# A fused recurrence, Fourier mixing and MLP kernel: the last row tile in two column parts, under new order tables

## The chip, the cores and the metric

The kernel runs on one core of one Trainium2 chip. A core has a matrix engine (PE, TensorE) whose weight loads (PEld) overlap its matmuls, a vector engine (DVE), a scalar engine (ACT), a general engine (POOL, GpSimd) and a queue engine (SP) that here issues transfers only. Matmul results go to eight PSUM banks. The metric is the device time of one execution in microseconds, the median of several runs.

## The reference

Four batches, eight heads, 768 time steps, 48 channels for each head, all in fp32. First a recurrence for each head, then a two-dimensional Fourier transform of which the real part is kept, a normalisation and a two-layer MLP with a residual.

```python
for t in range(S):
    kt, vt, rt, wt = (k[:, :, t].copy(), v[:, :, t].copy(), r[:, :, t].copy(), w[:, :, t].copy())
    cur = np.einsum('bhd,bhe->bhde', u[None] * kt, vt)
    y[:, :, t] = np.einsum('bhd,bhde->bhe', rt, state + cur)
    state = wt[:, :, :, None] * state + np.einsum('bhd,bhe->bhde', kt, vt)
...
X = np.fft.fft(x, axis=1)
X = np.fft.fft(X, axis=2)
mixed = np.real(X).astype(np.float32)
u = x + mixed
mu = np.mean(u, axis=-1, keepdims=True)
var = np.mean((u - mu) ** 2, axis=-1, keepdims=True)
un = (u - mu) / np.sqrt(var + 1e-06)
ch = np.maximum(un @ w_ch1, 0.0) @ w_ch2
return (u + ch).astype(np.float32)
```

## The kernel before

The work is written as a list of small operations, each with a kind and a number (`rl` 17 is the 18th ReLU). `op` (L63) records an operation with what it reads and writes; waits follow from that. Two tables then fix where and when it runs. `PLACES` holds a string of digits for some kinds: the digit at place n picks one of the engines that the call offers for operation n. `PLAN` holds a key for every operation; `schedule` (L100) sorts each engine's operations by key, and that is the engine's instruction order, so a key is a place in a queue and every engine works its queue strictly in order. `schedule` also walks through the orders once to give each PSUM tile a bank (L143 to L148): a bank is handed on when the last operation on its tile is through. `emit` (L194) sets the waits and, at the end, lets DVE wait for every output store (L261 to L265).

A batch has six chunks of 128 steps. `load` issues on SP the tiles w, k, r, v of a chunk (192 KB each, load number 4 x chunk + 0 to 3); `weights` issues the two MLP weight matrices on POOL (`wgt` 0 for W1, 1 for W2, L697 and L698), tied to a load of chunk 5.

`attention` works on one chunk: ACT takes logarithms (`Ln`) and exponentials (`ex`, `ew`, L739) of cumulative sums from PE (`tce`, `tci`); products go to POOL or DVE (`rk`, `rku`, `vtd`, `kh`) or read a bank on DVE (`rh`); `vb` casts v to bf16; PE transposes (`trr`, `trk`), the results are copied out by ACT or DVE (`rT`, `kT`, L785 and L786); PE forms the 128 x 128 products (`am`), DVE masks them (`ms`, L802); PE forms the state and the output (`sm`, `y`, for chunks 0 to 5 with the diagonal term by `yx`, L830), DVE scales the state (`st`), and `xc` copies the output out (L853, L854). `fe`, `fo` (L867, L870) fold the channels for the transform.

`mix` works on a batch: PE transforms along the sequence with 193 columns at a time (`sq`, L897), the results are copied (`hc`, L914 and L915, and `hr` from those); PE transforms along the channels (`dm`), DVE adds the input (`uf`, L955), takes statistics (`bs`, `ba`), `un` centres, PE transposes (`tr`), `ut` copies out. For batches 2 and 3 two of the six row tiles are mirrored by transfers instead, and `uf` is a sum of two SBUF tiles there, on DVE or POOL. Then, for each half batch q of three row tiles, 12 `m1` (three matmuls of 384 columns each, L998) with a ReLU each on ACT or DVE (`rl`, L1003 and L1004) make the hidden layer HT, and for each row tile three `m2` (four matmuls each, L1014) accumulate over the 12 blocks of HT into one bank. `ob` (L1020) scales by the inverse deviation and adds the residual on DVE, and `out` (L1024) stores the 192 KB tile from SP. Row tile 23 is the last of the run: its three `m2` are the last instructions of PE, its `ob` the last of DVE and its `out` the last transfer.

Until its real work is dense, PE is kept busy by matmuls on a zero tile (`beat`, L1040), 29 at the start and others in gaps that `fill_gaps` finds in the walk of `schedule`.

Of the kernel before, what the change touches and what calls it, by code (L numbers as in the profile page):

```python
# [7 lines left out]
ALU = mybir.AluOpType  # L8
# [24 lines left out]
class _Prog:  # L33
# [254 lines left out]
    def _topo(self):  # L288
# [3 lines left out]
        while n < len(self.ops):  # L292
# [18 lines left out]
    "tce": [2, 6, 17, 14, 32, 39, 67, 112, 81, 111, 153, 161, 170, 189, 203, 245, 246, 260, 275, 283, 325, 317, 338, 375],  # L311
    "tci": [3, 4, 8, 12, 34, 37, 49, 94, 92, 105, 145, 160, 171, 184, 199, 212, 234, 263, 272, 287, 343, 318, 329, 372],
    "tot": [7, 5, 10, 18, 36, 58, 97, 96, 110, 147, 175, 185, 200, 213, 242, 280, 288, 345, 327, 336],
    "trr": [9, 16, 22, 23, 43, 56, 76, 126, 116, 141, 165, 172, 183, 197, 222, 252, 268, 270, 285, 298, 361, 357, 367, 397],
    "trk": [13, 11, 20, 25, 47, 50, 71, 130, 122, 146, 164, 178, 192, 194, 235, 243, 255, 286, 305, 306, 360, 359, 364, 394],
    "sm": [15, 31, 40, 48, 64, 86, 131, 154, 168, 179, 187, 210, 254, 271, 284, 307, 322, 358, 386, 399],
    "am": [19, 24, 33, 30, 57, 62, 82, 137, 132, 151, 174, 182, 196, 204, 240, 257, 274, 296, 352, 311, 368, 370, 385, 401],
    "set": [0, 1, 4, 3, 5, 6, 5, 11, 13, 21, 23, 1, 2, 16, 22, 25, 28, 3, 4, 26, 27, 30, 34, 5, 6, 7, 14, 35, 19, 40, 18, 32,
           33, 50, 36, 45, 51, 41, 57, 39, 24, 12, 29, 17, 31, 21, 28, 27],
    "yx": [26, 38, 42, 44, 59, 66],  # L320
    "y": [29, 41, 45, 51, 65, 70, 129, 152, 150, 167, 181, 190, 207, 244, 262, 278, 292, 304, 373, 339, 374, 389, 398, 406],
    "beat": [35],
# [64 lines left out]
    "wgt": [28, 36],  # L387
    "ix": [47, 84],
    "dx": [88],
    "mg": [110, 109, 125, 124],  # L390
# [711 lines left out]
```

## Time and profile before

| | us |
|---|---|
| median of 3 runs | 192.83 (192.76 to 192.97) |
| the profiled execution | 193.89 |
| its span, first to last instruction | 192.1 |

| engine | busy us | share of the span | instructions |
|---|---|---|---|
| PE | 182.9 | 95% | 1803 |
| PEld | 120.9 | 63% | 1803 |
| DVE | 163.8 | 85% | 405 |
| ACT | 139.9 | 73% | 326 |
| POOL | 106.9 | 56% | 130 |

The profile is of one execution, whose own time stands beside its span; the span starts with the first instruction and leaves out what lies around it. Times in the views count from the start of the span. A row of the grouped view reads: line, engine, operation, output from inputs, shapes, count, then busy us and mean ns of one, then the idle time of the engine ahead of them and what ended it. The view by stretches gives the busy time of each engine in a stretch with the instruction count in brackets, then the clock granted to PE, DMA's mean share and its GB/s. The view of the chain that ended last gives start, length and what ran.

### The profile page before, as it was taken

The page shows a single profiled execution, that of the slowest core. Times are in us where ns is not written, and L with a number is a line of the kernel's source. Part 1 is how long each engine was busy: PE and PEld are TensorE (multiplying, and loading weights), DVE is VectorE, ACT ScalarE, POOL GpSimd, SP SyncE. Part 2 cuts the span into 40 slices and gives each one's busy share as a digit, 9 for nine tenths or more (in the row PEclk, how much of TensorE's full clock was granted, in tenths as well). Part 3 has the DMA queues.
Part 4 walks back from the last instruction along what each step waited for, and adds up shares of the span by engine and source line. Part 5 has one row for each costly group of instructions (what it writes and reads, how often), then busy time and mean ns, then how long its engine had stood idle before and what let it go on. Part 6 is the DMA issues. An engine that isn't in the chain of part 4 may idle for free.

```text
span 192.1 us, 4796 instructions
## 1 busy us (share of the span) xinstructions
PE 182.9 (95%) x1803; PEld 120.9 (63%) x1803; DVE 163.8 (85%) x405; ACT 139.9 (73%) x326; POOL 106.9 (56%) x130
## 2 busy tenths in 40 slices
PE   7798999998899999999999999999999999999993
PEld 5465668845567666767667577665666676666561
DVE  8698999899989999999999989898989947584532
ACT  4896997879988468879999777878875766473410
POOL 3139665745907967994999794694992301200000
PEclk9999999999999999999999999999999999999999
DMA  5998999999999896999979990156601022203303
GB/s 120 211 190 157 201 195 182 188 210 196 174 184 180 175 198 149 201 230 194 232 169 223 193 217 19 46 163 171 160 0 44 2 85 82 82 0 126 125 0 123
DMA packets 106109, 27.84 MB, mean 145 GB/s; under 512 B 100387, under 2 KB 105510, under 8 KB 106086
## 3 DMA queue, kind: packets, MB, share of 16 engines
q1 hardware_dynamic: 103878, 24.39, 59.1%
q0 software_dynamic: 2208, 3.15, 8.9%
q8 instruction: 14, 0.23, 0.5%
q14 instruction: 9, 0.07, 0.1%
HBM read 24.38 MB, written 5.51 MB: 156 GB/s over the span
## 4 chain that ended last, share of the span: by engine, by line
PE 76%; SPq 10%; DVE 8%; DMA 2%; issue 1%; ACT 1%; POOL 0%; DVEq 0%; POOLq 0%
PE bank L1014 24%; PE bank L998 22%; SPq L570 10%; PE bank L897 5%; PE bank L941 4%; PE bank L795 3%; PE bank L779 2%; PE bank L841 2%; DMA in_v<-in_v_dram 2%; PE bank L773 2%; PE bank L838 2%; PE bank L971 2%; DVE uf L955 2%; PE bank L720 1%; PE bank L815 1%; PE bank L812 1%
## 5 line engine op out<-in xcount | busy, mean ns | idle before, releaser
L1014 PE MATMUL bank<-w,ht 128*128 128x384 bf16 x288 | 54.8, 326 | 0.0
L998 PE MATMUL bank<-unt,w 128*128 128x384 bf16 x288 | 53.2, 326 | 0.2 <-ACT unt L979 0.2
L1003 ACT ACTIVATE ht<-bank 128x384 bf16<-128x384 f32 x79 | 36.3, 494 | 15.2 <-PE bank L998 14.9
L998 PEld LDWEIGHTS bank<-unt,w 128*128 128x128 bf16 x288 | 26.4, 97 | 17.4 <-DVE ah L802 0.9
L1014 PEld LDWEIGHTS bank<-w,ht 128*128 128x128 bf16 x288 | 26.8, 98 | 15.3 <-DVE fd L870 0.2
L802 DVE TENSOR_TENSOR ah<-bank,msk 128x512 bf16<-128x512 f32 x48 | 31.8, 681 | 1.5 <-PE bank L795 1.3
L540 POOL TENSOR_TENSOR rk<-in_r,in_k 128x384 f32<-128x384 f32 x23 | 23.2, 1010 | 14.6 <-DMA in_r<-in_r_dram 9.6
L540 POOL TENSOR_TENSOR vtd<-in_v,dc 128x384 f32<-128x384 f32 x23 | 19.3, 840 | 13.6 <-DVE dc L747 10.4
L540 POOL TENSOR_TENSOR rk<-rk,ub 128x384 f32<-128x384 f32 x20 | 20.1, 1011 | 0.6
L1020 DVE SCALAR_TENSOR_TENSOR osb<-bank,rstd,uf 128x384 f32<-128x384 f32 x24 | 14.6, 610 | 6.7 <-PE bank L1014 6.4
L540 POOL TENSOR_TENSOR kh<-in_k,e 128x384 bf16<-128x384 f32 x17 | 17.0, 1006 | 4.1 <-ACT e L739 4.0
L540 POOL TENSOR_TENSOR xf<-fd,ft 128x384 bf16<-128x384 f32 x13 | 12.8, 1003 | 7.9 <-DVE ft L870 5.6
L823 DVE TENSOR_TENSOR st<-bank,e 64x192 bf16<-64x192 f32 x40 | 14.1, 352 | 1.0 <-PE bank L815 0.4
L757 DVE TENSOR_TENSOR rh<-bank,in_r 128x384 bf16<-128x384 f32 x24 | 13.1, 546 | 1.0 <-ACT ktb L785 0.6
L554 ACT ACTIVATE un<-uf,agg 128x384 bf16<-128x384 f32 x20 | 12.0, 617 | 2.7 <-DVE agg L962 2.5
L853 ACT ACTIVATE x<-bank 128x384 f32<-128x384 f32 x20 | 9.8, 491 | 5.1 <-DVE bank L849 3.7
L785 ACT ACTIVATE rtb<-bank 128x512 bf16<-128x512 bf16 x20 | 12.0, 600 | 1.9 <-PE bank L773 1.9
L747 DVE TENSOR_REDUCE dc<-rk 128x8 f32<-128x384 f32 x24 | 12.8, 540 | 0.0
L960 DVE BATCH_NORM_STATS2 bst<-uf 128x6 f32<-128x384 f32 x24 | 12.7, 545 | 0.1
L979 ACT ACTIVATE unt<-bank 128x384 bf16<-128x384 f32 x20 | 9.2, 487 | 4.7 <-PE bank L971 4.4
L955 DVE TENSOR_TENSOR uf<-bank,x 128x384 f32<-128x384 f32 x20 | 10.6, 542 | 2.2 <-ACT mrow L948 1.8
L1004 DVE TENSOR_SCALAR ht<-bank 128x384 bf16<-128x384 f32 x17 | 9.0, 550 | 4.0 <-PE bank L998 4.0
(144 smaller groups left out, 390.3 us busy)
## 6 DMA issues: line engine op xcount, KB each, us to landing
in_w<-in_w_dram SPq DMA_DIRECT2D x24, 192.0 KB, 3.9
in_r<-in_r_dram SPq DMA_DIRECT2D x24, 192.0 KB, 4.0
in_k<-in_k_dram SPq DMA_DIRECT2D x24, 192.0 KB, 4.0
in_v<-in_v_dram SPq DMA_DIRECT2D x24, 192.0 KB, 3.9
out_dram<-osb SPq DMA_DIRECT2D x24, 192.0 KB, 2.2
w<-in_moe_w_ch_dram POOLq DMA_DIRECT2D x2, 1152.0 KB, 11.7
mirror<-uf SPq DMA_DIRECT2D x4, 192.0 KB, 1.8
uf<-mirror,ix POOLq DMA_INDIRECT x4, 3.9
```

The source lines that it names most:

```text
L540: return shared(lambda e: e.tensor_tensor(out=o, in0=a, in1=b, op=f))
L570: return e.dma_start(INB[x][i][:, :, :], src[x][b, :, c * CH:(c + 1) * CH, :].rearrange("h t d -> t h d"))
L747: op(("dc", n), ("dve", 542, lambda e: e.tensor_reduce(out=dc[:, :], in_=rk[:, :, :], axis=mybir.AxisListType.X, op=ALU.add)), r=[("RK", i ...
L757: op(("rh", n), ("dve", 551, lambda e: e.tensor_tensor(out=rh[:, :, 0:D], in0=ps(tce)[:, 0:DM].rearrange("t (h d) -> t h d", d=D), in1=rt[ ...
L802: op(("ms", 2 * n + x), ("dve", 682, lambda e, x=x: e.tensor_tensor(out=ah[:, x:H:2, :], in0=ps(ta[x])[:, :].rearrange("p (h t) -> p h t", ...
L823: op(("st", 2 * n + x), ("dve", 360, lambda e, x=x, pr=pr: e.tensor_tensor(out=s_out[pr, :, D * x:D * x + D], in0=ps(tds)[pr, 0:DM].rearra ...
L955: op(("uf", n), [("dve", 543, lambda e, kb=kb, t=t: e.tensor_tensor(out=uf[:, kb, :], in0=ps(t)[:, 0:DM], in1=xb[:, kb, 0:DM], op=ALU.add) ...
L960: op(("bs", n), ("dve", 549, lambda e, kb=kb, bs=bs: e.bn_stats(bs[:, :], uf[:, kb, :])), r=[("UF", i, kb)], w=[("BST", n % 4)])
L998: ins = e.matmul(ps(t)[:, 0:384], W1[:, m, 128 * j:128 * j + 128], unt[:, m, :], start=(m == 0), stop=(m == NM - 1))
L1003: ("act", 490, lambda e, j=j, t=t, ht=ht: e.activation(ht[:, j, :], ps(t)[:, 0:384], ACTF.Relu)),
L1014: ins = e.matmul(ps(t)[:, 0:DM], ht[:, j, 128 * x:128 * x + 128], W2[:, j, :], start=(j == 0), stop=(j == NJ - 1))
L1020: op(("ob", n), ("dve", 614, lambda e, kb=kb, t=t, o=o: e.scalar_tensor_tensor(out=o[:, :], in0=ps(t)[:, 0:DM], scalar=rstd[:, kb:kb + 1], ...
```

## The change

In `mix`, the set SPLIT names row tiles that are done in two column halves; it holds tile 23 alone. For it each half has a bank of its own: three `m2h` of four matmuls with 192 columns, an `obh` on DVE over 192 columns, and an `outh` from SP of 96 KB, each half with a semaphore. The keys of the six `m2h` put them in the order left, right, left, left, right, right (by thirds of the hidden layer).

The same diff adds a way to transpose by transfers (TDH), which is empty, so that the old branch runs everywhere; with it each ReLU gets a factor `sg`, here 1.0: on ACT as the scale, on DVE as a multiplication ahead of the maximum in the same instruction.

All tables of `PLAN` and `PLACES` are replaced. Of the keys only those that the text uses are shown here, the first line of each.

```diff
+    "m2h": [490, 492, 493, 491, 494, 495],
...
-    "load": [1, 5, 6, 7, 0, 4, 3, 16, 8, 10, 13, 14, 9, 11, 12, 22, 18, 19, 17, 23, 15, 24, 21, 28, 20, 27, 29, 25, 31, 35,
+    "load": [1, 4, 6, 8, 5, 7, 0, 12, 3, 11, 10, 16, 9, 14, 13, 21, 19, 17, 18, 24, 15, 23, 22, 29, 20, 26, 27, 28, 31, 34,
...
-    "kh": [49, 48, 55, 59, 78, 81, 29, 37, 35, 136, 48, 51, 56, 59, 69, 70, 73, 85, 87, 94, 106, 100, 105, 117],
+    "kh": [44, 42, 57, 60, 78, 85, 35, 38, 36, 41, 50, 54, 60, 62, 69, 71, 77, 84, 89, 96, 106, 103, 107, 120],
...
-    "ew": [15, 13, 20, 26, 39, 47, 54, 77, 70, 80, 112, 118, 127, 136, 144, 151, 166, 181, 197, 202, 236, 227, 233, 257],
+    "ew": [13, 11, 19, 25, 43, 44, 54, 81, 70, 78, 112, 120, 126, 136, 146, 152, 166, 181, 198, 205, 239, 227, 235, 260],
...
-    "wgt": [28, 36],
+    "wgt": [33, 40],
...
 PLACES = {
-    "rk": "000000000100000000000000",
-    "rku": "100000010000100000000010",
-    "vtd": "100000000000000000000000",
-    "vb": "100000000000000000000000",
-    "kh": "000000000100000000000000",
-    "rT": "000000000110000000110000",
-    "kT": "010100000100000010001010",
-    "xc": "000000110000001000000100",
-    "hc": "110000100010",
-    "hr": "200020200212",
-    "uf": "000000000000000011000000",
-    "un": "000100000000000000001101",
-    "rl": "110000011000000000000000010000000000100001100001000001000000000000000000010000010000100101011000",
+    "rk": "000000000001000000000000",
+    "rku": "000000000000100000000000",
+    "vtd": "000000100000000000010000",
+    "vb": "100000100000000000000000",
+    "kh": "000000000000000000000000",
+    "rT": "110000001110000000001010",
+    "kT": "000000010000000010000011",
+    "xc": "000000000000001001000100",
+    "hc": "001000110010",
+    "hr": "122022222112",
+    "uf": "000000000000000011000011",
+    "un": "000010000000000000110011",
+    "rl": "010100000101010000000000000100000000100010101001010000100000000111000010110000110010001100111010",
...
@@ -961,24 +962,28 @@
                r=[("UF", i, kb)], w=[("BST", n % 4)])
             op(("ba", n), ("dve", 173, lambda e, kb=kb, bs=bs: e.bn_aggr(agg[:, kb, :], bs[:, :])),
                r=[("BST", n % 4)], w=[("AGG", i, kb)])
+            hf = kb // 3
+            unt = UNT[(2 * b + hf) % 2][:, :, 128 * (kb % 3):128 * (kb % 3) + 128]
             op(("un", n), [("act", 616, act(un[:, :], uf[:, kb, :], ACTF.Identity, scale=-1.0, bias=agg[:, kb, 0:1])),
                            ("dve", 412, ts(un[:, :], uf[:, kb, :], -1.0, agg[:, kb, 0:1], ALU.mult, ALU.add))],
                r=[("UF", i, kb), ("AGG", i, kb)], w=[("UN", n % 3)])
-            tu = g.tile("f")
-
-            def tr(e, un=un, tu=tu):
-                for m in range(NM):
-                    ins = e.matmul(ps(tu)[:, 128 * m:128 * m + 128], un[:, 128 * m:128 * m + 128], NIDW[:, 128:256])
-                return ins
-            op(("tr", n), ("pe", 171, tr), r=["NIDW", ("UN", n % 3)], w=[tu])
-            hf = kb // 3
-            unt = UNT[(2 * b + hf) % 2][:, :, 128 * (kb % 3):128 * (kb % 3) + 128]
-
-            def flat(t):
-                return ps(t)[:, 0:DM].rearrange("p (m t) -> p m t", t=128)
-            op(("ut", n), [("act", 490, lambda e, tu=tu, unt=unt: e.activation(unt, flat(tu), ACTF.Copy)),
-                           ("dve", 548, lambda e, tu=tu, unt=unt: e.tensor_copy(out=unt, in_=flat(tu)))],
-               r=[tu], w=[("UNT", (2 * b + hf) % 2, kb % 3)])
+            if 2 * b + hf in TDH:
+                op(("tt", n), ("sp", 60, lambda e, un=un, unt=unt: e.dma_start_transpose(unt, un[:, :])),
+                   r=[("UN", n % 3)], w=[("UNT", (2 * b + hf) % 2, kb % 3)], sem="tt%d" % (n % 3), nbytes=192000, fix=2000.0)
+            else:
+                tu = g.tile("f")
+
+                def tr(e, un=un, tu=tu):
+                    for m in range(NM):
+                        ins = e.matmul(ps(tu)[:, 128 * m:128 * m + 128], un[:, 128 * m:128 * m + 128], NIDW[:, 128:256])
+                    return ins
+                op(("tr", n), ("pe", 171, tr), r=["NIDW", ("UN", n % 3)], w=[tu])
+
+                def flat(t):
+                    return ps(t)[:, 0:DM].rearrange("p (m t) -> p m t", t=128)
+                op(("ut", n), [("act", 490, lambda e, tu=tu, unt=unt: e.activation(unt, flat(tu), ACTF.Copy)),
+                               ("dve", 548, lambda e, tu=tu, unt=unt: e.tensor_copy(out=unt, in_=flat(tu)))],
+                   r=[tu], w=[("UNT", (2 * b + hf) % 2, kb % 3)])
             if kb % 3 == 2:
                 sl = slice(kb - 2, kb + 1)
                 op(("lv", 2 * b + hf), ("act", 290, lambda e, sl=sl: e.activation(lnv[:, sl], agg[:, sl, 1], ACTF.Ln,
@@ -990,6 +995,7 @@
         for hf in range(2):
             q = 2 * b + hf
             unt, ht = UNT[q % 2], HT[q % 2]
+            sg = -1.0 if q in TDH else 1.0
             for j in range(NJ):
                 t = g.tile("f")
 
@@ -1000,13 +1006,34 @@
                     return ins
                 op(("m1", q * NJ + j), ("pe", 488, f), r=[("UNT", q % 2, x) for x in range(3)] + ["W1"], w=[t])
                 op(("rl", q * NJ + j), [
-                    ("act", 490, lambda e, j=j, t=t, ht=ht: e.activation(ht[:, j, :], ps(t)[:, 0:384], ACTF.Relu)),
-                    ("dve", 552, lambda e, j=j, t=t, ht=ht: e.tensor_scalar(
-                        out=ht[:, j, :], in0=ps(t)[:, 0:384], scalar1=0.0, scalar2=None, op0=ALU.max))],
+                    ("act", 490, lambda e, j=j, t=t, ht=ht, sg=sg: e.activation(ht[:, j, :], ps(t)[:, 0:384], ACTF.Relu, scale=sg)),
+                    ("dve", 552, lambda e, j=j, t=t, ht=ht, sg=sg: e.tensor_scalar(
+                        out=ht[:, j, :], in0=ps(t)[:, 0:384], scalar1=sg, scalar2=0.0, op0=ALU.mult, op1=ALU.max))],
                    r=[t], w=[("HT", q % 2, j)] + (["IDF"] if q == 1 else []))
             for x in range(3):
                 kb = 3 * hf + x
                 n = b * NC + kb
+                o = OSB[n % 3]
+                if n in SPLIT:
+                    for y in range(2):
+                        cs_ = slice(DM // 2 * y, DM // 2 * y + DM // 2)
+                        t = g.tile("f")
+                        for jq in range(3):
+                            def f(e, x=x, jq=jq, t=t, ht=ht, cs_=cs_):
+                                for j in range(4 * jq, 4 * jq + 4):
+                                    ins = e.matmul(ps(t)[:, 0:DM // 2], ht[:, j, 128 * x:128 * x + 128], W2[:, j, cs_],
+                                                   start=(j == 0), stop=(j == NJ - 1))
+                                return ins
+                            op(("m2h", 3 * y + jq), ("pe", 345, f),
+                               r=[("HT", q % 2, j) for j in range(4 * jq, 4 * jq + 4)] + ["W2"], w=[t])
+                        op(("obh", y), ("dve", 350, lambda e, kb=kb, t=t, o=o, cs_=cs_: e.scalar_tensor_tensor(
+                            out=o[:, cs_], in0=ps(t)[:, 0:DM // 2], scalar=rstd[:, kb:kb + 1], in1=uf[:, kb, cs_],
+                            op0=ALU.mult, op1=ALU.add)),
+                           r=[t, ("RSTD", i, hf), ("UF", i, kb)], w=[("OSB", n % 3, y), ("OSB", n % 3)])
+                        op(("outh", y), ("sp", 60, lambda e, kb=kb, o=o, cs_=cs_: e.dma_start(
+                            out[b, kb * 128:(kb + 1) * 128, cs_], o[:, cs_])),
+                           r=[("OSB", n % 3, y)], w=[("out", b, kb, y)], sem="outh%d" % y, nbytes=64 * DM * 4, fix=800.0)
+                    continue
                 t = g.tile("f")
                 for jq in range(3):
                     def f(e, x=x, jq=jq, t=t, ht=ht):
@@ -1016,7 +1043,6 @@
                         return ins
                     op(("m2", 3 * n + jq), ("pe", 650, f),
                        r=[("HT", q % 2, j) for j in range(4 * jq, 4 * jq + 4)] + ["W2"], w=[t])
-                o = OSB[n % 3]
                 op(("ob", n), ("dve", 614, lambda e, kb=kb, t=t, o=o: e.scalar_tensor_tensor(
                     out=o[:, :], in0=ps(t)[:, 0:DM], scalar=rstd[:, kb:kb + 1], in1=uf[:, kb, :],
                     op0=ALU.mult, op1=ALU.add)),
@@ -1030,6 +1056,8 @@
     KBANK = (0, 1, 2, 3, 4, 5)
     BEATS, BEAT0 = 3, 29
     MIRROR = (2, 3)
+    TDH = ()
+    SPLIT = (23,)
 
     op(("set", 0), ("act", 1290, lambda e: e.preload_act_table_set("trig_and_small")), w=["TRIG"])
     n_set[0] = 1
```

More of the change, by code (lines that the diff above doesn't have):

```diff
@@ L310 @@
     "ux": [1],
[L311 to L321, printed above, removed]
@@ new lines @@
+    "set": [0, 0, 4, 5, 3, 9, 1, 9, 11, 16, 18, 1, 2, 12, 17, 19, 22, 3, 4, 20, 23, 24, 27, 5, 6, 7, 6, 28, 13, 25, 14, 10,
+           33, 51, 32, 51, 45, 36, 56, 41, 30, 26, 31, 15, 29, 20, 35, 27],
+    "yx": [24, 34, 32, 46, 61, 69],
+    "y": [30, 39, 44, 47, 66, 70, 128, 151, 148, 167, 181, 191, 207, 243, 260, 274, 293, 304, 370, 334, 381, 388, 397, 407],
+    "beat": [36],
[38 rows of a table added]
+    "zero": [1, 38, 8, 7, 13, 34, 2, 35, 6, 8, 48, 2, 40, 19, 37, 25, 12, 22, 5, 7, 0, 3],
+    "zero0": [4],
+    "row": [21],
[15 rows of a table added]
```

39 lines of the change are left out of this document (22 added, 17 removed), and 112 rows, old and new, of the table PLAN.

## The prediction

> **What bounds the kernel now.** I read the page's shares first, then the busy time by stretches, then the chain of work that ended last, and last the tail by hand.
>
> ```profile
> span 192.1 us, 4796 instructions
> 0.00:23.00 23.00, 19.73 (x192) 13.33 (x193) 19.62 (x70) 17.53 (x39) 11.11 (x25) 1.00 0.88 174
> 23.00:50.00 27.00, 25.51 (x282) 17.50 (x280) 25.83 (x64) 23.22 (x53) 17.34 (x19) 1.00 1.02 194
> 50.00:60.00 10.00, 9.12 (x96) 5.95 (x96) 9.29 (x21) 8.52 (x21) 4.17 (x6) 1.00 1.21 184
> 60.00:189.06 129.06, 128.53 (x1238) 84.11 (x1236) 108.44 (x253) 90.67 (x215) 74.33 (x83) 1.00 0.55 128
> 189.06:192.10 3.04, 0.00 (x0) 0.00 (x0) 0.62 (x1) 0.00 (x0) 0.00 (x0) 1.00 0.21 77
> 9.60:60.00 50.40, 47.20 (x524) 31.80 (x525) 47.68 (x112) 43.18 (x101) 29.91 (x35) 1.00 1.03 188
> L1040 PE MATMUL bank<-wz 128*128 128x256 bf16 x71 | 11.0, 304 | 1.1 <-DVE wz L551 1.1
> ```
>
> The columns are the stretch, its length, then busy time of PE, weight loads, DVE, ACT and POOL, the granted clock, DMA's share and its GB/s. There are three stages with three limits. From 60 us to 189.06 PE is busy 128.53 of 129.06 us: it loses 0.53 us, so nothing on another engine can shorten this stage, and a new order can only lose there. Up to 60 us PE also looks busy, but 11.0 us of its 182.9 are the 71 empty matmuls that keep it warm (L1040), and it idles besides. There DVE is busy 47.68 of 50.40 us and the DMA engines show 1.03 of their time: both limit the head. The last 3.04 us are one eviction and one store. The clock is 1.00 throughout.
>
> ```profile
> 20.65 0.77 SPq L570
> 21.46 3.98 DMA in_v<-in_v_dram
> 25.58 0.84 POOL vtd L540
> 183.10 5.86 PE bank L1014 x36
> 189.06 0.62 DVE osb L1020
> 189.70 0.33 SPq L1024 DMA_DIRECT2D out_dram<-osb  x1
> 190.50:190.60 0.10, 0.00 (x0) 0.00 (x0) 0.00 (x0) 0.00 (x0) 0.00 (x0) 1.00 0.48 169
> 191.10:191.20 0.10, 0.00 (x0) 0.00 (x0) 0.00 (x0) 0.00 (x0) 0.00 (x0) 1.00 0.17 46
> ```
>
> The chain that ended last says the same: loads issued one behind the other on SP up to the v tile of chunk 3 (landed 25.4 us), then a mix of DVE and PE, then PE without a gap, at the end 36 matmuls of the last three row tiles, one eviction of 0.62 us, and the store, issued at 189.70, with its data moving from 190.5 to about 191.15 and the end at 192.10.
>
> **The tail, the named part of the change.** The last tile's 12 matmuls of 384 columns become 24 of 192, its eviction and its store two of each.
>
> ```profile
> 153.41 0.67 PE bank L897 x8
> L897 PEld LDWEIGHTS bank<-cs,xf 128*128 128x128 bf16 x54 | 4.8, 97 | 0.7
> L955 DVE TENSOR_TENSOR uf<-bank,x 128x384 f32<-128x384 f32 x20 | 10.6, 542 | 2.2 <-ACT mrow L948 1.8 <-ACT uf L948 0.3
> L867 DVE TENSOR_TENSOR ft<-bank,x 128x193 f32<-128x193 f32 x9 | 3.1, 345 | 0.0
> L1020 DVE SCALAR_TENSOR_TENSOR osb<-bank,rstd,uf 128x384 f32<-128x384 f32 x24 | 14.6, 610 | 6.7 <-PE bank L1014 6.4
> ```
>
> PE: 5.86/36 = 0.163 us for one matmul now, 12 of them 1.95 us. The nearest row for 192 columns is the sequence transform with 193: 8 in 0.67 us, 0.084 each, and each with a weight load of its own, as here. 24 x 0.084 = 2.01 us, **+0.06**. Ends: 0 (half of 0.163 each), and +0.38 if each narrow matmul had to wait out its 0.097 us weight load (24 x 0.097 = 2.33). I take the row of the same shape.
>
> The Trainium skill, "TensorE: Matmul & The Clock Gate", section "Back-to-back issue gap", speaks against the split: in pairs of weight load and matmul it gives about 81 ns at 128 columns and 131 ns at 512. Interpolated, an estimate, that is 89 ns at 192 and 114 at 384, and the split would cost 24 x 89 - 12 x 114 ns = 0.77 us. The trace does not agree: 163 ns at 384 columns lies above both of its figures; the isolated gap that the same section gives, 2.5 ns plus one column per 1/2.4 ns (82 and 162 ns), fits both rows.
>
> Eviction: a two-tensor operation out of a bank takes 542 ns for 384 elements and 345 for 193, so 1.03 ns for each. 610 - 192 x 1.03 = 0.41 us for the last half: **-0.20** (-0.27 at best, if it costs 345). The first half's eviction starts when its last matmul is through. The keys order the six parts as left, right, left, left, right, right, so eight matmuls (0.67 us) still follow; the 0.41 us are over before PE ends and DVE is free for the second. Cover gone, it would cost 0.41.
>
> Store: 2.42 us from the eviction's end (189.68) to the end of the span. The data take about 0.65 of it; half the bytes save 0.33 at best, and nothing if the 128 rows count and not their bytes. **-0.20**, between the two, nearer to the bytes since the engines showed full use in that burst. The first half's store is issued before the second's eviction is done, and SP needs 0.33 us for it, so the second isn't queued behind it. The closing wait on DVE for one more store that landed earlier is nothing. Tail: 0.06 - 0.20 - 0.20 = **-0.34**; ends -0.60 and +0.18.
>
> **The rest of the diff: another order and other engines for the whole run.** Every table of keys changes. The PE sequence stays nearly the same in its large steps, and its work is the same; SP, DVE, ACT and POOL change. What decides is the head. For chunks 0 to 9 and the first batch's mixing the digits take from DVE: two products rku (chunks 0, 7), one kh (9), two copies xc (6, 7), two evictions kT less, one hc; they add three rT, one vb (6), one more ReLU, one hr. The others there (vtd, rk, un) change places one for one.
>
> ```profile
> L540 DVE TENSOR_TENSOR rk<-rk,ub 128x384 f32<-128x384 f32 x4 | 2.2, 549 | 1.1 <-POOL rk L540 1.1
> L540 DVE TENSOR_TENSOR kh<-in_k,e 128x384 bf16<-128x384 f32 x1 | 1.1, 1096 | 0.0
> L854 DVE COPY x<-bank 128x384 f32<-128x384 f32 x4 | 2.2, 544 | 0.0
> L786 DVE COPY ktb<-bank 128x512 bf16<-128x512 bf16 x6 | 2.5, 414 | 0.0
> L915 DVE CAST hcs<-bank 128x386 bf16<-128x386 f32 x4 | 2.3, 597 | 1.7 <-PE bank L897 1.7
> L754 DVE CAST vb<-in_v 128x384 bf16<-128x384 f32 x1 | 0.4, 354 | 0.0
> L1004 DVE TENSOR_SCALAR ht<-bank 128x384 bf16<-128x384 f32 x17 | 9.0, 550 | 4.0 <-PE bank L998 4.0
> L544 DVE TENSOR_SCALAR nidw<-idw 128x384 bf16<-128x384 bf16 x1 | 0.2, 196 | 0.0
> ...
> 45.74 0.54 DVE L747 TENSOR_REDUCE dc<-rk 128x8 f32<-128x384 f32 x1
> 46.20 0.55 DVE L960 BATCH_NORM_STATS2 bst<-uf 128x6 f32<-128x384 f32 x1
> ```
>
> Taken: 2 x 0.55 + 1.10 + 2 x 0.54 + 2 x 0.41 + 0.60 = 4.70. Added: 3 x 0.41 + 0.35 + 0.55 + 0.20 = 2.33. DVE is relieved of 2.4 us of the head's 47.68. But the kh's 1.10 is twice what the same kind of operation takes elsewhere (0.55), and neighbours overlap (45.74 to 46.20 is 0.46 for an operation of 0.54), so I count 1.7. (hr, which the trace doesn't show on DVE at this size, goes by the copy of 384 bf16 elements at 0.196.) It goes mostly to POOL, which is busy 29.91 of 50.40 there. How much reaches the end is bounded: nothing, if the loads set the head (DMA 1.03), or even a loss if their new order is worse; 1.7 if DVE does. The loads do gain at the one place that the chain names: the v tile of chunk 3 moves from place 22 to 21 on SP, one issue, about 0.8 us (20.65 to 21.46). I take **-0.6**, a third of DVE's relief, since two limits share the head.
>
> Against it stands a charge for the dense stage. It loses 0.53 us now; a different order of 250 DVE and 215 ACT instructions will hardly lose less. I add **+0.3**: half as much again of what is lost now; ends 0 and 1.5.
>
> One wait I could place. W2's load is issued on POOL, and one more operation, kh of chunk 7, now stands ahead of it:
>
> ```profile
> 44.36 0.49 ACT L739 ACTIVATE e<-bank 128x388 f32<-128x388 f32 x1
> 44.73 0.50 ACT L724 ACTIVATE bank<-bank 128x384 f32<-128x384 f32 x1
> 44.61 1.62 PE L998 MATMUL bank<-unt,w 128*128 128x384 bf16 x9 [0.25 <-ACT unt L979]
> 45.40 1.00 POOL L540 TENSOR_TENSOR rk<-in_r,in_k 128x384 f32<-128x384 f32 x1 [4.93 <-DMA in_k<-in_k_dram]
> 47.30 1.12 POOL L698 DMA_DIRECT2D w<-in_moe_w_ch_dram  x1
> DMA to landing us min/median/max: 12.5/12.5/12.5
> 61.80 3.41 PE L1014 MATMUL bank<-w,ht 128*128 128x384 bf16 x20
> ```
>
> Before, that kh stood behind the issue. It needs the k tile (in at 45.4) and the exponential ew7, which moves from first to fourth of four on ACT (44.36 plus three times 0.37, then 0.49: done at 46.0). Then kh, rk at 1.00 each: the issue at 48.0 and not 47.30. W2 lands 12.5 us after it, 59.8 to 60.9 before, and the first m2 runs at 61.8: 0.9 to 2.0 us of slack. 0.7 later is still covered; with a head 0.6 earlier it eats at most 0.4, which is in the 0.3 above.
>
> The rest costs nothing by place: the two additions uf that move to POOL in the last batch, and 11 more ReLUs on DVE (17 to 28), belong, but for one ReLU, to the later batches; over the dense stage DVE has 129.06 - 108.44 = 20.6 us free.
>
> **Sum.** -0.34 - 0.6 + 0.3 = -0.64. The profiled execution took 193.89 us, of which 192.10 are the span; the span would be 191.46, that execution 193.25. The median of the runs is 192.83, 1.06 below the profiled one, and the same difference puts the new median at **192.2 us**.
>
> **Rivals.**
> - Only the tail counts (14 in 100): the head is set by the loads, DMA at 1.03 speaks for it, the 95% of DVE against it. 192.83 - 0.34 = 192.5.
> - DVE alone sets the head (14): all 1.7 come through, 192.83 - 0.34 - 1.7 + 0.3 = 191.1. The back-to-back DVE from 23 to 50 us (25.83 of 27) speaks for it.
> - W2 late (14), on the slower side: the issue waits for the k tile of chunk 7, which came in just at 45.4 after 4.93 us of waiting. If that tile or ew7 comes 2.5 us later, the issue is at 50.5, 3.2 late, and PE, in order, stops for 1.2 to 2.3 us at the first m2. It decides from an issue at about 49.2 on. 192.2 + 1.6 = 193.8. Against it: both feeders are early in the new order.
> - ReLUs held on DVE (10): a ReLU behind other DVE work holds a bank and the m2 behind it. It decides when two operations of 0.6 us stand ahead, since some two m2 groups (1.3 us) cover it; if five or six of the 11 new ones lose 0.3 us each, 193.9.
> - Narrow matmuls paced by the weight load (6): +0.38 for +0.06, 192.2 + 0.32 = 192.5. The 0.084 of L897 speaks against it. (This is the mechanism of the skill's sustained gap, in the section named above.)
>
> The forecast as summed has 42. A measurement of this kernel tells about 0.2% (0.4 us) from no change. Faster: most of 42, all of 14, a part of the 192.5 cases: 0.55. Within: 0.15. Slower: W2, ReLUs, and a worse load order: 0.30. The forecast's own range is 191.6 to 192.8; with the rivals on both sides 190.9 to 193.8.
>
> **What would show it.** Tail: m2h parts at 0.33 to 0.34 us each, last eviction 0.41, end 2.2 us after it. Head: first m1 earlier than 44.61 by half a microsecond, DVE's share in 9.6 to 60 us lower or the same work done sooner; W2's issue near 48. Dense stage: PE loses under 1 us from the first m2 to the last. Wrong if PE shows a wait above 1 us behind 60 us, or the head ends no earlier.

## The result and the profile after

| | median us | runs | ratio to before, 95% interval |
|---|---|---|---|
| before, beside it | 192.8 | 4 | |
| changed kernel | 194.81 (194.22 to 197.12) | 4 | 1.0115 (1.007 to 1.016) |
| changed kernel, on another chip, before at 192.22 | 194.8 (194.3 to 195.74) | 6 | 1.0136 (1.0103 to 1.0169) |

The change costs a little over 1%, about 2.2 us; the forecast was a gain of 0.6 us. The page of the changed kernel, then its busy time by stretches, with the columns as before:

```profile
span 193.0 us, 4812 instructions
L1068 PE MATMUL bank<-wz 128*128 128x256 bf16 x74 | 12.8, 324 | 1.5 <-DVE wz L552 1.5
```

```profile
0.00:23.00 23.00, 20.77 (x188) 13.51 (x188) 18.98 (x67) 16.48 (x37) 13.33 (x30) 1.00 0.94 181
23.00:50.00 27.00, 25.51 (x282) 17.22 (x283) 25.39 (x65) 23.08 (x54) 13.84 (x15) 1.00 0.97 184
50.00:60.00 10.00, 9.10 (x92) 5.58 (x91) 9.18 (x19) 7.30 (x18) 6.30 (x7) 1.00 1.21 184
60.00:189.06 129.06, 128.15 (x1250) 85.07 (x1248) 113.04 (x261) 87.38 (x209) 77.78 (x85) 1.00 0.55 128
189.06:193.00 3.94, 1.06 (x13) 0.83 (x11) 0.83 (x2) 0.00 (x0) 0.00 (x0) 1.00 0.29 100
9.60:60.00 50.40, 47.25 (x518) 31.12 (x516) 46.80 (x110) 40.30 (x95) 31.02 (x37) 1.00 1.03 188
```

Read against the rows of before: DVE is busy for less in the head, 46.80 us instead of 47.68 from 9.6 to 60 us, and POOL took work on, 31.02 for 29.91. But less was done by then: 518 instructions on PE instead of 524, 110 on DVE instead of 112. A kernel with before's order and the split tile (`r1_split_only`, below) is further on still, with 559 and 114:

```profile
9.60:60.00 50.40, 48.61 (x559) 33.13 (x560) 48.15 (x114) 43.77 (x104) 31.54 (x37) 1.00 1.03 189
```

So the lower figure of DVE is work that is late, not yet a relief. PE's busy time hides the delay, since the empty matmuls fill its idle time: 74 with 12.8 us instead of 71 with 11.0. From 60 to 189.06 us PE loses 129.06 - 128.15 = 0.91 us, where it lost 0.53.

One caution on the pair of profiles. The profiled execution of before was itself about 1 us longer than its median (193.89 against 192.83), and `r1_split_only` profiled at a span of 190.3, not 192.1, though the medians differ by 0.2. So the comparisons below go against that one. Even so, one kernel profiled twice (r10 and r18, on two chips) ended its last matmul at 186.75 and at 188.20 us: a difference of about a microsecond between two profiles counts only where a wait inside the trace explains it, or where it returns in several kernels.

The tail, first by the chain that ended last, then by its timeline:

```profile
188.14 1.99 PE bank L1024 x24
```

```profile
187.98 2.14 PE L1024 MATMUL bank<-w,ht 128*128 128x192 bf16 x24
189.57 0.42 DVE L1029 SCALAR_TENSOR_TENSOR osb<-bank,rstd,uf 128x192 f32<-128x192 f32 x1 [0.70 <-PE bank L1024]
190.01 0.99 SPq L1033 DMA_DIRECT2D out_dram<-osb  x2
190.23 0.42 DVE L1029 SCALAR_TENSOR_TENSOR osb<-bank,rstd,uf 128x192 f32<-128x192 f32 x1 [0.24 <-PE bank L1024]
```

24 narrow matmuls take 1.99 us (0.083 each, 0.33 for a group of four), against 12 x 0.163 = 1.95. The last eviction takes 0.42 instead of 0.62. It ends at 190.65, 2.35 us ahead of the span's end, where it was 2.42: half the bytes saved 0.07 of the store. The data themselves did move in less time, 0.40 us instead of 0.65, here the stretches in which the DMA engines are active, before and after:

```profile
190.50:191.15 0.65, 0.00 (x0) 0.00 (x0) 0.00 (x0) 0.00 (x0) 0.00 (x0) 1.00 0.84 303
191.50:191.90 0.40, 0.00 (x0) 0.00 (x0) 0.00 (x0) 0.00 (x0) 0.00 (x0) 1.00 0.76 242
```

But the span ends 1.10 us behind them, where before had 0.95. DVE now waits for five store semaphores at the end instead of three; whether that is the reason, no run here shows. From the first matmul of the last tile to the end it is 193.0 - 188.14 = 4.86 us, where before had 192.1 - (183.10 + 24 x 0.163) = 5.09. The tail gained 0.23, and the split alone shows the same 4.86 (190.3 - 185.44).

The first hidden-layer matmul, the first of the second layer, and the issue of W2 on POOL with its landing:

```profile
45.60 0.65 PE L1004 MATMUL bank<-unt,w 128*128 128x384 bf16 x3
62.06 0.82 PE L1041 MATMUL bank<-w,ht 128*128 128x384 bf16 x4
```

```profile
49.31 1.08 POOL L699 DMA_DIRECT2D w<-in_moe_w_ch_dram  x1
DMA to landing us min/median/max: 12.4/12.4/12.4
```

The head ends later, 45.60 for 44.61, or for 43.98 in the split alone. W2 was issued at 49.31, later than the 48.0 that I had worked out, and landed at 61.7, just ahead of its first use.

### The profile page after: what moved, and what is told of

Read it like the earlier page. It is cut to its first block, busy times and chain, and to the rows that moved or that the text cites. A ratio compares the mean times of both kernels' runs of the same rounds, so it can differ in the third digit from the quotient of the medians.

```text
span 193.0 us, 4812 instructions
## 1 busy us (share of the span) xinstructions
PE 184.6 (96%) x1818; PEld 122.2 (63%) x1818; DVE 167.4 (87%) x411; ACT 134.2 (70%) x315; POOL 111.3 (58%) x136
## 4 chain that ended last, share of the span: by engine, by line
PE 57%; DVE 28%; DMA 4%; ACT 3%; issue 3%; POOL 3%; SPq 0%; DVEq 0%; POOLq 0%; ACTq 0%
PE bank L1004 17%; PE bank L1041 14%; PE bank L898 5%; DVE ah L803 4%; PE bank L942 4%; DVE rh L758 3%; DVE st L824 3%; DMA uf<-mirror,ix 3%; PE bank L796 2%; DVE dc L748 2%; PE bank L831 2%; DVE bank L850 2%; DVE bst L961 2%; DMA mirror<-uf 2%; PE bank L780 2%
## 5 line engine op out<-in xcount | busy, mean ns | idle before, releaser
L1041 PE MATMUL bank<-w,ht 128*128 128x384 bf16 x276 | 52.0, 326 | 0.0
L1009 ACT ACTIVATE ht<-bank 128x384 bf16<-128x384 f32 x68 | 31.2, 495 | 19.4 <-PE bank L1004 19.1
L1041 PEld LDWEIGHTS bank<-w,ht 128*128 128x128 bf16 x276 | 25.4, 98 | 14.5
L541 POOL TENSOR_TENSOR rk<-rk,ub 128x384 f32<-128x384 f32 x23 | 23.2, 1013 | 2.3 <-DVE rk L541 1.6
L541 POOL TENSOR_TENSOR vtd<-in_v,dc 128x384 f32<-128x384 f32 x22 | 18.1, 829 | 8.6 <-DVE dc L748 7.2
L541 POOL TENSOR_TENSOR xf<-fd,ft 128x384 bf16<-128x384 f32 x17 | 16.7, 1002 | 5.5 <-DVE ft L871 3.0
L1010 DVE TENSOR_SCALAR ht<-bank 128x384 bf16<-128x384 f32 x28 | 14.8, 548 | 4.3 <-PE bank L1004 3.9
L1046 DVE SCALAR_TENSOR_TENSOR osb<-bank,rstd,uf 128x384 f32<-128x384 f32 x23 | 13.9, 608 | 4.6 <-PE bank L1041 4.3
L1068 PE MATMUL bank<-wz 128*128 128x256 bf16 x74 | 12.8, 324 | 1.5 <-DVE wz L552 1.5
L725 ACT ACTIVATE bank<-bank 128x384 f32<-128x384 f32 x24 | 11.4, 485 | 3.8 <-PE bank L721 3.8
L786 ACT ACTIVATE ktb<-bank 128x512 bf16<-128x512 bf16 x20 | 11.8, 598 | 2.3 <-PE bank L780 2.2
L555 ACT ACTIVATE un<-uf,agg 128x384 bf16<-128x384 f32 x19 | 11.4, 618 | 2.5 <-DVE agg L963 2.5
```

Source lines behind the costliest of these rows:

```text
L541: return shared(lambda e: e.tensor_tensor(out=o, in0=a, in1=b, op=f))
L1009: ("act", 490, lambda e, j=j, t=t, ht=ht, sg=sg: e.activation(ht[:, j, :], ps(t)[:, 0:384], ACTF.Relu, scale=sg)),
L1010: ("dve", 552, lambda e, j=j, t=t, ht=ht, sg=sg: e.tensor_scalar(out=ht[:, j, :], in0=ps(t)[:, 0:384], scalar1=sg, scalar2=0.0, op0=ALU.mu ...
L1041: ins = e.matmul(ps(t)[:, 0:DM], ht[:, j, 128 * x:128 * x + 128], W2[:, j, :], start=(j == 0), stop=(j == NJ - 1))
L1046: op(("ob", n), ("dve", 614, lambda e, kb=kb, t=t, o=o: e.scalar_tensor_tensor(out=o[:, :], in0=ps(t)[:, 0:DM], scalar=rstd[:, kb:kb + 1], ...
L1068: return e.matmul(ps(tw)[:, 0:256], WZ[:, 0:128], WZ[:, :])
```

## The experiments

Ratios are to before on the same chip, in five groups of kernels (r1 to r4, r5 to r7, r8 to r11, r12 to r15, r16 to r18). Between groups, the ratio of like kernels differs by some tenths of a per cent, so a verdict rests on kernels of one group.

### Split or order

```diff
 # r1_split_only: the changed code with before's tables, and
+    "m2h": [490, 492, 493, 491, 494, 495],
+    "obh": [404, 405],
+    "outh": [126, 127],
 # r2_order_only: the changed kernel with its tables, the last tile whole
-    SPLIT = (23,)
+    SPLIT = ()
```

> The tables of before, with only row tile 23 split (its six parts, two evictions and two stores take the places that the whole tile had). Theory 1 (the split itself gains what the prediction said, the new order loses): 192.5 us, 0.2 to 0.5 below before, and as steady as before (within 0.3 us). Theory 2 (the split costs, by the narrow matmuls or the two stores): above 192.9.

> The tables of the changed kernel with row tile 23 whole, in the places of its parts. Theory 1 (order loses, split gains): 195.1 us, about 0.3 above the changed kernel, and as unsteady as that one (spread of 2 us or more). Theory 2 (the split costs): at or below 194.0.

The split alone 0.9995 (0.998 to 1.0011), the new order alone 1.0156 (1.012 to 1.0193), both near their first theory. The named part of the change is harmless, and 0.23 us is too little for the runs to tell. The loss is all in the tables.

### One operation each

The new order puts the cast of chunk 0's v ahead of everything that DVE does for the first chunks. DVE of the changed kernel, then of the split alone; the bracket is the idle time ahead and what ended it:

```profile
7.87 0.27 DVE L552 MEMSET lb<- 128x256 uint32 x1
10.65 0.62 DVE L755 CAST vb<-in_v 128x384 bf16<-128x384 f32 x1 [2.51 <-DMA in_v<-in_v_dram]
11.26 0.22 DVE L552 MEMSET st<- 128x192 uint32 x1
11.40 0.84 DVE L545 TENSOR_SCALAR nidw<-idw 128x384 bf16<-128x384 bf16 x1
12.16 0.54 DVE L762 TENSOR_TENSOR kh<-bank,in_k 128x384 bf16<-128x384 f32 x1
```

```profile
9.77 0.56 DVE L539 TENSOR_TENSOR rk<-rk,ub 128x384 f32<-128x384 f32 x1 [1.15 <-POOL rk L539]
10.29 0.11 DVE L550 MEMSET rh<- 128x64 uint32 x1
10.37 0.55 DVE L746 TENSOR_REDUCE dc<-rk 128x8 f32<-128x384 f32 x1
10.84 0.55 DVE L756 TENSOR_TENSOR rh<-bank,in_r 128x384 bf16<-128x384 f32 x1
```

The cast waits 2.51 us for its tile with the queue behind it; in the old order DVE has done a product, a reduction and the first decayed r by 11.4 us. The loads have a share in this wait: the new load order issues the v tile of chunk 0 at 6.48 us, the old one at 5.42. Besides, some DVE operations with all operands in SBUF are drawn out: `nidw` 0.84 us for 0.20 in the old order. Two more in the changed kernel, each with the POOL row beside it:

```profile
51.39 1.41 DVE L541 TENSOR_TENSOR vtd<-in_v,dc 128x384 f32<-128x384 f32 x1
51.37 1.01 POOL L541 TENSOR_TENSOR rk<-in_r,in_k 128x384 f32<-128x384 f32 x1
...
76.91 1.39 DVE L541 TENSOR_TENSOR rk<-rk,ub 128x384 f32<-128x384 f32 x1
76.89 1.00 POOL L541 TENSOR_TENSOR kh<-in_k,e 128x384 bf16<-128x384 f32 x1 [0.78 <-ACT e L740]
```

Such a product takes 0.55 on DVE alone; these two, started beside a POOL product, end 0.41 to 0.42 us after that one's end.

```diff
 # r3_vb0_later: the changed kernel, the cast behind the second kh
-    "vb": [39, 23, 34, 39, 50, 58,
+    "vb": [44.5, 23, 34, 39, 50, 58,
 # r4_before_vb0_first: the kernel before, the cast ahead of rku of chunk 0
-    "vb": [47, 31, 33, 48, 55, 56,
+    "vb": [41.5, 31, 33, 48, 55, 56,
 # r5_no_collision: as r3, with un of tile 4 on ACT, vtd of chunk 6 and rku of chunk 12 on POOL
-    "rku": "000000000000100000000000",
-    "vtd": "000000100000000000010000",
-    "un": "000010000000000000110011",
+    "rku": "000000000000000000000000",
+    "vtd": "000000000000000000010000",
+    "un": "000000000000000000110011",
 # r6_split_relieved: as r1, with kh of chunk 9 on POOL and un of tile 3 on ACT
-    "kh": "000000000100000000000000",
-    "un": "000100000000000000001101",
+    "kh": "000000000000000000000000",
+    "un": "000000000000000000001101",
 # r7_rku12_pool: the changed kernel, rku of chunk 12 on POOL
-    "rku": "000000000000100000000000",
+    "rku": "000000000000000000000000",
```

> The changed kernel with one operation moved: the cast vb of chunk 0 goes on DVE from ahead of the first kh to behind the second, so that DVE does not wait 2.5 us for the v tile and the two small operations behind it run before POOL starts. Theory 1a (that wait and the collision behind it set the head back): 193.6 us, first m1 near 44.6. Theory 1b (the head is set elsewhere, by loads or by later DVE work): within 0.3 us of the changed kernel, first m1 near 45.5.

> The kernel before with the cast vb of chunk 0 moved on DVE ahead of the first rku, where it waits for the v tile as in the changed kernel. Theory 1a (that wait sets the head back): 193.5 us or more, first m1 0.7 later than 44.6. Theory 1b: within 0.3 us of before.

> The changed kernel with vb of chunk 0 moved as before and three more SBUF-only operations taken off DVE where they ran beside POOL: un of row tile 4 to ACT, vtd of chunk 6 and rku of chunk 12 to POOL. Theory 1 (each DVE operation that is drawn out beside POOL delays the end by as much): 194.46 less 0.84 (un), 0.83 (rku) and the operations' own 0.4 to 0.5 each, so 192.3 to 193.0. Theory 2 (the new order is slow by its order, not by these operations): 194.0 or more.

> The tables of before with row tile 23 split and its two drawn-out DVE operations moved: un of row tile 3 to ACT, kh of chunk 9 to POOL. Theory 1: 192.58 less some 0.5 (kh, drawn out by 0.57) plus 0.45 to 1.0 (the two off DVE, un drawn out by 1.04 in some executions): 191.3 to 192.0. Theory 2 (DVE does not set the end there): within 0.3 of 192.58.

> The changed kernel with one operation moved: rku of chunk 12 from DVE (1.39 us there at 76.9 us) to POOL. Theory 1: DVE gets 1.3 us free and PE loses 0.5 to 0.9 us less between 70 and 90 us; 194.0. Theory 2 (PE is the limit from 60 us on and hides it): 194.8.

| kernel | median us | ratio, 95% interval |
|---|---|---|
| `r3_vb0_later` | 194.46 | 1.0092 (1.007 to 1.0115) |
| `r4_before_vb0_first` | 193.78 | 1.0039 (1.002 to 1.0058) |
| `r5_no_collision` | 193.78 | 1.0055 (1.0032 to 1.0078) |
| `r6_split_relieved` | 192.96 | 1.001 (0.9993 to 1.0028) |
| `r7_rku12_pool` | 193.72 | 1.004 (1.0021 to 1.006) |

The early cast alone makes the old order 0.4% slower (r4), so to place it early costs time. The way is only in part that of the changed kernel: under the old load order the cast waits 0.57 us, not 2.51, and the product behind it then runs beside a POOL product (9.74 to 10.84 us) and is drawn out:

```profile
9.19 0.80 DVE L754 CAST vb<-in_v 128x384 bf16<-128x384 f32 x1 [0.57 <-DMA in_v<-in_v_dram]
9.91 1.34 DVE L540 TENSOR_TENSOR rk<-rk,ub 128x384 f32<-128x384 f32 x1
```

Taking the cast out of the new order, alone or with three drawn-out operations (r3, r5), leaves over half a per cent; both came out between what their two theories said. r7 came near its first theory's 194.0. Taking the two drawn-out ones out of the old order gained nothing (r6): a miss for the idea that drawn-out operations are the loss wherever they stand. In r5 another wait shows between 44 and 60 us, PE held for a bank by a ReLU that comes late:

```profile
PE bank L1004 <- ACT ht L1009: 0.8, 2, 0.5
```

### Which stretch

Each engine's queue is cut at a time and continued in the other table's order: everything that has started by then in the one kernel, then the rest as the other has it, engines included, the keys numbered anew. One of the strings that move, as the kernels have it:

```diff
 # the changed kernel, then r8, r9, r10, r12, r13
     "rku": "000000000000100000000000",
+    "rku": "100000010000100000000000",
+    "rku": "000000000000100000000010",
+    "rku": "100000010000000000000000",
+    "rku": "000000010000100000000010",
+    "rku": "100000000000100000000010",
```

> Before's order and engines for everything that started ahead of 60 us, the changed kernel's for everything after, the last tile split. The changed kernel stands at 1.0115 of before, the split alone at 0.9995. Theory 1 (about 1 us is lost ahead of 60 us, by the v cast placed first and by the late ReLUs, and about 1 us at 76.9 us, where the product r*k*u of chunk 12 now runs on DVE beside a POOL product): what is left is the one at 76.9 us, 1.004 to 1.007, and TensorE stands level with the split-only kernel up to 75 us. Theory 2 (all of it is lost ahead of 60 us, and the 76.9 us product is slow only in the wake of that): 0.999 to 1.002. Theory 3 (the rest of the order is the slow one): 1.009 to 1.013.

> The reverse: the changed kernel's order and engines up to 60 us, before's for all the rest, the last tile split. Theory 1: the head's part alone, 1.004 to 1.008, with the loss in the profile all ahead of 60 us. Theory 2: 1.010 to 1.013. Theory 3: 0.999 to 1.002.

> As the one with before's order up to 60 us, and the r*k*u product of chunk 12 on POOL as in before. Theory 1: both causes gone, so level with the split-only kernel, 0.998 to 1.002. Theory 2: the same as without the move. Theory 3: still over 1.006.

> The changed kernel with two of its about 750 operations put back: the v cast of chunk 0 behind the second kh product (alone it gave 1.0092 against 1.0115) and the r*k*u product of chunk 12 on POOL (alone 1.004). If the two savings add: 1.001 to 1.003. If the later ReLUs of 45 to 54 us take up what the v cast frees, as they seemed to with the product of chunk 12 still on DVE: 1.003 to 1.005, with TensorE's waits for a bank at 45 to 54 us in the profile.

> The changed kernel's order and engines for what started ahead of 20 us, before's for the rest, the last tile split. In the profile of the run with the changed order up to 60 us, TensorE stood 2.2 us behind the split-only kernel from 20 to 45 us and 3.3 us from 56 us on. Theory 1 (the first 20 us are lost for good): 1.006 to 1.010, TensorE 1.5 to 2.5 us behind at 40 us and the same at the end. Rival (what is lost there is made up while TensorE waits later anyway, and only 45 to 56 us count): 0.999 to 1.002.

> Before's order up to 20 us, the changed kernel's from there to 60 us, before's again behind it, the last tile split. Theory 1: only the 1.1 us of 45 to 56 us, 1.002 to 1.005. Rival: nearly the whole loss, 1.008 to 1.013.

> As the one with the changed order up to 20 us, with the v cast of chunk 0 behind the second kh product. If the cast's 2.5 us of waiting is what the first 20 us cost: 0.999 to 1.002. If it is about half of it, as the profile of the changed kernel with the cast alone put back suggests (1.0 us behind at 40 us instead of 1.7): 1.003 to 1.006. If it is beside the point: as without it.

> The changed kernel, on the chip of the other three. Its loss should be about that of the run with the changed order to 20 us and that with it from 20 to 60 us together: 1.009 to 1.014. If the two together give less than two thirds of it, the causes work on each other, and the split by stretches doesn't hold.

| kernel | new order in | median us | ratio, 95% interval |
|---|---|---|---|
| `r8_head_old` | 60 us on | 192.57 | 1.002 (0.9994 to 1.0047) |
| `r9_head_new` | up to 60 us | 194.32 | 1.0118 (1.0083 to 1.0153) |
| `r10_head_old_rku12` | 60 us on, rku of chunk 12 on POOL | 191.58 | 0.9985 (0.9963 to 1.0008) |
| `r11_vb0_rku12` | all, two operations put back | 194.03 | 1.0108 (1.0075 to 1.0141) |
| `r12_new_to_20` | up to 20 us | 194.32 | 1.0094 (1.006 to 1.0128) |
| `r13_new_20_60` | 20 to 60 us | 193.34 | 1.0055 (1.0031 to 1.0078) |
| `r14_new_to_20_vb0` | up to 20 us, the cast put back | 193.61 | 1.0063 (1.0041 to 1.0084) |
| `r15_after_beside` | all | 194.8 | 1.0136 (1.0103 to 1.0169) |

The head carries the loss: the new order up to 60 us alone costs as much as the whole change, the new order behind it next to nothing. Within the head, the first 20 us cost 0.94% and 20 to 60 us 0.55%, together 1.49 where the whole has 1.36. Putting the cast back in the first 20 us takes off 0.3% (r14 against r12), with intervals that overlap. In time, r8 and r9 came out as their second theory had it, r10, r12 and r15 as forecast; r13 and r14 lie just above the ranges given, and r11 missed both of its own. The chain's last row, the 24 narrow matmuls, shows how an early loss is carried through. In order the split alone, r9, r13, r14, r8 and r10:

```profile
185.44 1.99 PE bank L1022 x24
```

```profile
188.70 1.99 PE bank L1001 x24
```

```profile
186.54 1.99 PE bank L1001 x24
```

```profile
186.96 1.99 PE bank L1001 x24
```

```profile
185.66 1.99 PE bank L1001 x24
```

```profile
184.76 1.99 PE bank L1001 x24
```

Their first transposing matmul of the mixing starts at 40.5, 42.8, 41.1, 42.1, 40.2 and 40.2 us. r14 is 1.6 us behind the split alone there and 1.5 at the end, with nothing else changed behind 20 us: 120 us of dense work on PE make up nothing in this pair (by the ratios it is 1.3 us). r9 is 2.3 behind at that place and 3.3 at the end, in an execution that was itself 1 us longer than its median; 0.7 of the last microsecond is lost at the drawn-out `vtd` and the ReLU behind it, for which PE waits, in r9 as in the changed kernel. The row of r9:

```profile
PE bank L981 <- DVE ht L987: 0.7, 1, 0.7
```

r8 and r10 differ in one product, drawn out in r8 just as in the changed kernel, though it runs 2.5 us earlier there:

```profile
74.41 1.39 DVE L518 TENSOR_TENSOR rk<-rk,ub 128x384 f32<-128x384 f32 x1
74.39 1.00 POOL L518 TENSOR_TENSOR kh<-in_k,e 128x384 bf16<-128x384 f32 x1 [0.77 <-ACT e L717]
```

In the profiles its price is 185.66 - 184.76 = 0.90 us; by the runs 0.35%, with intervals that overlap. The traces show the wait: PE stands for a decayed r that DVE makes behind the product. In the changed kernel:

```profile
PE bank L898 <- DVE rh L758: 0.8, 1, 0.8
```

This wait, 0.5 to 0.8 us, is in all five profiles in which the product is drawn out (the changed kernel and r15, r2, r3, r8) and in none of the six with it on POOL. Under the new order, PE takes 127.9 to 128.2 us from the first matmul of the second layer to its last with the product on DVE (the changed kernel and r15, r2, r3) and 127.1 to 127.5 with it on POOL (r5, r7, r11, r17); the split alone takes 127.3. So the price is some 0.7 us, in the dense stage. In r11, though, with that product on POOL and the cast put back, little was gained in all (1.0108), against r7's 1.004 in another group. How much of the total such a move brings is therefore not settled.

### What is left of the first 20 us

With the cast put back, 0.6% stay. One reason is in DVE's queue of r14: without the cast, the next operation there, the first `kh`, waits 1.62 us for an exponential from ACT, as it does in r3 and r16.

```profile
10.08 0.56 DVE L739 TENSOR_TENSOR kh<-bank,in_k 128x384 bf16<-128x384 f32 x1 [1.62 <-ACT e L713]
```

Besides, in r14 the first masked product starts behind a copy that the new tables moved from ACT to DVE (`rT` of chunk 1). r16 puts that copy back on ACT; r17 does the same in r11; r18 is r10 once more. PE of r14, then of r16:

```diff
 # r16_rT1_act
-    "rT": "110000000110000000110000",
+    "rT": "100000000110000000110000",
 # r17_three_back
-    "rT": "110000001110000000001010",
+    "rT": "100000001110000000001010",
```

```profile
16.16 0.40 PE L773 MATMUL bank<-rtb,ktb 48*128 48x128 bf16 x8 [0.34 <-DVE rtb L764]
```

```profile
15.43 0.40 PE L773 MATMUL bank<-rtb,ktb 48*128 48x128 bf16 x8
...
16.73 0.40 PE L751 MATMUL bank<-idw,rh 128*128 128x128 bf16 x4 [0.30 <-DVE rh L735]
```

> The changed order up to 20 us with the v cast of chunk 0 put back (1.0063), and now also the copy of chunk 1's transposed r on ACT, behind the first copy of transposed k there, as in before. If that copy is what is left of the first 20 us: the first masked product at about 15.2 us instead of 16.16, and 1.000 to 1.003. If the next copy or cast in DVE's queue holds PE just as long: 1.004 to 1.007.

> The changed kernel with three operations put back: the v cast of chunk 0 behind the second kh product, the r*k*u product of chunk 12 on POOL, the copy of chunk 1's transposed r on ACT. If the prices found one by one add (0.3, 0.4 and up to 0.6 per cent off 1.0136): 1.000 to 1.004. If what is freed ahead of 20 us is lost again at the ReLUs of 45 to 54 us: 1.005 to 1.010.

> Before's order up to 60 us, the changed kernel's behind it, the r*k*u product of chunk 12 on POOL, the last tile split: 0.9985 in the first measurement. If it is faster than before by the tail's quarter of a microsecond and what the later order brings: 0.996 to 0.999.

r16 gave 1.006 (1.0037 to 1.0084), r17 1.0095 (1.0058 to 1.0133), r18 0.9986 (0.9966 to 1.0006): r16 and r17 as their second alternative had it, r18 as forecast. The masked product does start 0.73 us earlier, and PE then waits for the next thing in DVE's queue, a decayed r. Not all of the 0.73 is the copy's: in r14's execution an operation ahead of it (`cs`) was drawn out to 1.03 us, in r16's it took 0.31; in r3, with the copy on DVE and `cs` at 0.30, the masked product starts at 15.75. r16's first transposing matmul is at 41.7 us, 0.4 ahead of r14's, and the ratio is the same within the noise (1.006 for 1.0063). None of the operations tried holds the rest; the three together in the new order take about a third off (1.0095 for 1.0136, in two groups). There another limit shows that the prediction had among its rivals: in r17's profile PE waits 0.69 us for W2 at the first matmul of the second layer, since the head is earlier and W2, landing 13.9 us after its issue at 48.22, is not.

```profile
62.29 0.81 PE L1041 MATMUL bank<-w,ht 128*128 128x384 bf16 x4 [0.69 <-DMA w<-in_moe_w_ch_dram]
```

The best version, r10 and r18, stands at 0.9985 and 0.9986 in two groups, at the edge of what these runs can tell from before.

## Why the prediction was wrong

**Tail: right, but for the store.** -0.34 forecast, -0.23 found. The narrow matmuls went by the 0.084 us row (+0.04 for +0.06) and not by the 0.77 us estimated from the Trainium skill, "TensorE: Matmul & The Clock Gate", section "Back-to-back issue gap"; the eviction by -0.20. The store was mis-sized: -0.07 for -0.20. Its data took 0.25 us less, of the 0.33 that half the bytes could save at best; most of it was lost again behind the last data.

**Head: the step that failed.** It read: "I take -0.6, a third of DVE's relief, since two limits share the head". Neither the gain nor the relief came; r9 puts the head at +1.2%, 2.3 us. With the new order up to 60 us and the old one behind it (r9), DVE has three instructions fewer over the whole run than the split alone, and is busy for longer. The pages of the split alone and of r9:

```profile
PE 182.7 (96%) x1815; PEld 121.7 (64%) x1815; DVE 163.0 (86%) x406; ACT 139.4 (73%) x326; POOL 107.0 (56%) x130
PE 183.3 (95%) x1818; PEld 121.3 (63%) x1818; DVE 164.5 (85%) x403; ACT 138.7 (72%) x325; POOL 108.2 (56%) x134
```

What was taken off DVE is more than made up by operations drawn out while POOL is at work, which the sum priced at what they take alone: in r9's execution the first cast, `nidw`, `ss`, `un` and `vtd` take some 3 us more together. And I priced the work that leaves an engine, not the places of what stays. DVE takes its queue strictly in order, and in the first 20 us every engine waits for the others. A shorter list in a worse order ends later: the cast's 2.51 us of waiting, the product that used to run on DVE in that time and is now on POOL, the reduction that used to follow it (at 10.37 us, now at 14.86), the copy taken over from ACT. In the stretch from 9 to 20 us, the split alone and then the changed kernel:

```profile
9.00:20.00 11.00, 10.22 (x121) 6.89 (x123) 10.17 (x24) 9.53 (x26) 7.43 (x10) 1.00 0.96 188
```

```profile
9.00:20.00 11.00, 10.56 (x111) 6.91 (x110) 9.27 (x22) 8.21 (x23) 9.28 (x13) 1.00 1.00 193
```

DVE and ACT are busy for less and do less, POOL is busy for more because it has what DVE had. PE shows more busy time with ten instructions fewer, since the empty matmuls count: 40 with 5.50 us of the 10.56, against 23 with 3.49 of the 10.22. The sentence on the lower bound, "even a loss if their new order is worse", was written for the loads alone and without a size. It looked at the v tile of chunk 3 only, and that of chunk 0 came to be issued 1.06 us later. The order of the loads is part of the first 20 us; it was not tried by itself, so its share against DVE's order and the choice of engines is open.

**Dense stage: right in sign, too small, and not in kind.** +0.3 forecast as a charge for any new order; PE loses 0.91 us instead of 0.53 in the same stretch, from the first matmul of the second layer to PE's end it is 128.07 us for the split alone's 127.28, +0.8, and r8 against r1 is +0.25%, 0.5 us. It is mostly one product beside POOL, and without it (r5, r7, r10) the charge is gone.

**W2:** the issue came at 49.31 rather than 48.0, past the point from which I had it decide; the whole kernel was late by then, so it landed 0.4 us ahead of its first use and held nothing. It did hold PE in r17, by 0.69 us, once the head was earlier. **ReLUs on DVE** cost 0.7 us in one place, in the way of that rival but behind a product drawn out beside POOL, and not in five or six. **Narrow matmuls paced by the weight load:** no.

That the loss lies in the head's tables, order and engines together, is shown by r8 and r9. That an early cast costs time is shown by r4 in the old order; in the new one r14 against r12 only suggests it. How the rest of the first 20 us is shared among the moved operations and loads stays open.

## What to carry to other kernels

A drop in an engine's busy time in a fixed stretch can be work that is late; it is no gain until the trace shows that the same instructions start earlier; where every queue is strict and engines feed each other in a chain, look at what stands behind an operation whose input arrives late. When a change comes with new order tables, cut the tables at a time and splice old and new: two runs showed which stretch carries the loss, where putting single operations back had not. Ahead of a dense stage that hardly waits, a microsecond lost was not made up in any run here.

## What the runs showed of the hardware

A DVE product with both inputs in SBUF, started within 0.02 us of a POOL product of the same kind, took 1.39 to 1.41 us instead of 0.55 in three places of two kernels, and ended 0.41 to 0.42 us after POOL's. In r4 one started 0.17 us after POOL's product, took 1.34 and ended 0.41 after it too. So its end goes by the end of the POOL product and not by its own start, as if it were held until POOL is through. The Trainium skill says so in "SBUF — State Buffer", section "SBUF: two separate sides": the two engines share one pair of ports under an exclusive lock for the whole instruction, which a DVE operation with two SBUF inputs also needs against a POOL operation that reads SBUF. These rows agree. Planned at 0.55, such a product costs some 0.85 more where the two start together; whether two operations meet depends on when POOL's input lands: `cs` took 1.03 us in r14 and 0.31 in r16, with the same DVE operations ahead of it, POOL's first product having started at 8.37 and at 9.08 us.

A store of half the bytes over the same 128 rows ended 0.07 us sooner, of 2.42, though its data moved in 0.40 us instead of 0.65.
